# Two layers of attention with a memory: reads split in halves and put ahead of the value sums, low parts and feature sums on GpSimd, clipping on ScalarE

## The chip, the cores and the metric

One of the eight NeuronCores of a Trainium2 chip runs the whole program. The metric is the device time of one execution in microseconds (us), as a median over runs. The core has five engines, each with its own instruction stream that it works off in order: TensorE (PE, with its weight loads shown apart as PEld), VectorE (DVE), ScalarE (ACT), GpSimd (POOL) and SyncE (SP, which here only issues transfers and passes on syncs). They share an on-chip memory (SBUF); TensorE writes its results to eight banks of PSUM, from which VectorE and ScalarE read them.

## The reference

A sequence of 2048 rows of 512 features goes through four residual layers, A, B, A, B. Both have 32 heads of width 16. A is a linear attention with softmax features. B, the layer that the change touches, works on four segments of 512 rows one after the other:

```python
phi = lambda t: where(t > 0, t + 1.0, exp(t))
for s in range(4):                                   # segments of 512 rows
    logits = einsum("bhqd,bhkd->bhqk", qs, ks) * 0.25 + mask      # causal
    a_dot = einsum("bhqk,bhkd->bhqd", softmax(logits), vs)
    pq = phi(qs)
    a_mem = einsum("bhld,bhde->bhle", pq, M) / (einsum("bhld,bhd->bhl", pq, z)[..., None] + 1e-6)
    o = g * a_mem + (1 - g) * a_dot                  # g = sigmoid(beta), per head
    pk = phi(ks)
    M = M + einsum("bhld,bhle->bhde", pk, vs)        # the memory
    z = z + pk.sum over rows
```

In every segment but the first the queries read the memory of the segments before; in every segment but the last the keys and values are written to it. The result is in float32.

## The kernel before

**Number format.** Matrix products of wide operands are made of two parts of each operand, a rounded "hi" and the remainder "lo" (hi·hi + hi·lo + lo·hi). So every projected tile needs a cast (hi, ScalarE) and a subtraction (lo).

**Layer B's steps.** `LayerB.steps` writes out the order of the work by hand. A segment's 32 heads are 4 chunks `c` of 8 heads, a chunk is 2 halves, so a segment has 8 groups `m` of four heads, a layer 32. Each group takes five steps `k`; I call the five steps of a group's place a *turn*. The tables FIRST, GAPS, LAST and FINAL (first segment, middle ones, last of layer 1, last of layer 2) have one row per turn and one cell per step: `5.2` is step 2 of turn 5. The entries are jobs: `Q`, `V`, `O` (projections of queries and keys, of values, output), `a` (a read of the memory), `t`, `m` (the two parts of a write), `fin` (normalization of a group's value sums), `max`, `cv`, `n`, `ln` and others; `/6` means six pieces of such a job, and `+` means the next segment's. The order in which the program issues instructions to an engine is kept (`Ordered`, `held`), so an instruction that waits holds up all that stand behind it on its engine.

In each step the program issues, in this order: one of five products of logits of the group (`attend`), one of five sets of products for the row maxima of a group two turns ahead (`maxima`), functions that were put off to this step (`self.at`), stacking transfers (`stack`, in steps 2 and 4), in step 0 the value sums of the group before (`weighted`), and then the jobs of the table's cell.

- `attend`: TensorE writes logits to the tile `lg` (one buffer of two banks), ScalarE takes its exponential into a tile `P` (128 x 1024), and GpSimd sets what lies above the diagonal to zero (`affine_select`; 128 x 256 once or twice in steps 0 to 3, 128 x 512 in step 4).
- `maxima`: products in the banks `mx` and `my`, in steps 2 and 4 in two banks of the pool `g`; VectorE takes masked maxima (CUSTOM_DVE, then DVE_READ_ACCUMULATOR into `mxs`).
- `weighted`: 32 small matmuls `g<-P,v` in a bank of `g`, key blocks in the order 0, 3, 1, 2. Block 2 comes from the exponential of step 4. ScalarE copies the result out as `U`.
- `proj_pair`: queries and keys of one chunk, in steps 1 to 4 of turns 0, 1, 4 and 6, into two banks of `g`. Its matmuls come as two halves of rows that change places by syncs over SP. At the end ScalarE copies both out (`raw`, tile `tb`), and `projected` puts off the rest: `parts` (hi, lo) and `features` (phi). So the parts and the features of the projections fall into turns 1, 2, 5 and 7 (and the first step of the turn after).
- `reads`: two halves per chunk, each 64 matmuls `g<-mem,tb` in a bank of `g` and a normalization on VectorE into `ot`, to which `finish` adds the value sums.

The pool `g` has four banks (`G = 4`). They serve value sums, reads, projections, transposes and the maxima of steps 2 and 4. All this is issued through the helpers at lines 155 (every engine but TensorE), 177 (matmul) and 181 (transpose), so the profile shows tiles rather than lines.

In the kernel before, phi is made so: ScalarE `e = exp(raw)`; GpSimd `e = min(e, 1)`; then for keys GpSimd `raw = max(raw, 0)` and `e = e + raw`, for queries VectorE `e = max(raw, 0) + e` in one instruction, two steps later. With the projection's end in step 4, the query's parts, features and sum come 2, 4 and 6 steps later, the key's parts and features 3 and 5.

Of the kernel before, what the change touches and what calls it, by code (L numbers as in the profile page):

```python
# [7 lines left out]
F32 = mybir.dt.float32  # L8
# [56 lines left out]
7.0 m3 a0+ a0+ max fin | 7.1 V+/6 w | 7.2 V+/6 n        | 7.3 V+/6 n | 7.4 V+/6 w  # L65
# [12 lines left out]
0.0 a1 a1 max fin | 0.1 Q2/6 n cv3    | 0.2 Q2/6 n        | 0.3 Q2/6 n | 0.4 Q2/6  # L78
1.0 max turn fin | 1.1 Q3/6          | 1.2 Q3/6 n        | 1.3 Q3/6 | 1.4 Q3/6
2.0 max turn ln fin | 2.1 O/6          | 2.2 O/6           | 2.3 O/6 | 2.4 O/6  # L80
3.0 max turn turn fin ln | 3.1 O/6     | 3.2 O/6           | 3.3 O/6 | 3.4 O/6
4.0 a2 a2 max ln ln fin | 4.1 v/2 cv0  | 4.2 v/2           | 4.3 v/2 cv1 | 4.4 v/2
5.0 a3 a3 max fin | 5.1 v/2           | 5.2 v/2           | 5.3 v/2 | 5.4 v/2
6.0 max fin pre | 6.1 cv2         | 6.2 P/4           | 6.3 P/9 | 6.4 P/5 v/1
# [3 lines left out]
0.0 a1 a1 max fin | 0.1 Q2/6 cv3      | 0.2 Q2/6          | 0.3 Q2/6 | 0.4 Q2/6  # L88
1.0 max turn turn fin | 1.1 Q3/6       | 1.2 Q3/6          | 1.3 Q3/6 | 1.4 Q3/6
2.0 max fin | 2.1 O/6 cv0       | 2.2 O/6           | 2.3 O/6 | 2.4 O/6  # L90
3.0 a2 a2 max fin | 3.1 O/6           | 3.2 O/6           | 3.3 O/6 | 3.4 O/6
4.0 max turn turn fin | 4.1 O/6 cv1    | 4.2 O/6           | 4.3 O/6 | 4.4 O/6
5.0 a3 a3 max fin | 5.1 O/6           | 5.2 O/6           | 5.3 O/6 | 5.4 O/6
6.0 max fin pre | 6.1 cv2         | 6.2 P/4           | 6.3 P/9 | 6.4 P/5
# [7 lines left out]
def interleave_kernel(ctx, tc, x_in, a_wqkv, a_wphi, a_wo, b_wq, b_wk, b_wv, b_wo, b_beta,  # L102
# [878 lines left out]
    class LayerB:  # L981
# [53 lines left out]
        def proj_pair(self, s, c):  # L1035
# [344 lines left out]
        def steps(self, side, after, table_end):  # L1380
# [88 lines left out]
            for k in range(BEGIN, R * N + 1):  # L1469
# [110 lines left out]
```

## Time and profile before

| | |
|---|---|
| median of 3 runs | 1369.1 us (1363.52 to 1370.22) |
| profiled execution | 1368.14 us, of which the span is 1366.4 |
| granted TensorE clock, mean | 0.992 |
| PE busy | 1294.7 us (95%) |
| DVE busy | 1089.9 us (80%) |
| ACT busy | 809.1 us (59%) |
| POOL busy | 738.4 us (54%) |

In a row of the profile's groups stand: line, engine, operation, out<-in by the program's names with the shapes, count | busy time in us, mean duration in ns | idle time of the engine just before them in us, and what ended it. In the rows in order of time stand: start and duration in us, engine, line, operation, out<-in, shapes, count, and in brackets the idle time before and who ended it. A wait for several semaphores is put down to the one that the profile takes for the last. A matmul's end is modelled, and matmuls overlap.

The tile `lg` belongs to the logits, `mxs` to the maxima, `tb` to projected rows and features, `ta` to hi and lo, `mem` to the memory.

### The profile page before, as it was taken

What the parts mean: (1) busy time and instruction counts of PE and PEld (TensorE: products, weight loads), DVE (VectorE), ACT (ScalarE), POOL (GpSimd) and SP (SyncE); (2) the same over time, 40 slices, a digit from 0 to 9 for tenths busy, and PEclk for the clock granted to TensorE, in tenths of its full rate; (3) what the DMA queues carried; (4) which work ended last, traced back from release to release, by engine and by line L of the source; (5) the groups of instructions that cost most, each with busy time, mean ns of one, the idle gap of its engine ahead of it and who ended that gap; (6) DMA issues with size and microseconds to landing.
All of it is one profiled execution on the core that took longest, in us unless ns stands there. A gap on an engine that the chain in (4) does not pass through costs nothing.

```text
span 1366.4 us, 41853 instructions
## 1 busy us (share of the span) xinstructions
PE 1294.7 (95%) x16552; PEld 997.1 (73%) x16552; DVE 1089.9 (80%) x3327; ACT 809.1 (59%) x1202; POOL 738.4 (54%) x1084
## 2 busy tenths in 40 slices
PE   7999989999999999999999998999999999999987
PEld 6887868777667767767668886886767777677665
DVE  4766778778888989888767676787789889888885
ACT  5556345546777667667644433463667766766654
POOL 1568766426658558445324355563366666765443
PEclk9999999999999999999999998999999999999999
DMA  6398437534555544546351103655446554543432
GB/s 204 101 335 262 161 125 226 183 95 124 170 175 142 144 123 130 144 135 172 103 179 39 63 33 124 212 166 156 137 136 184 150 152 110 142 139 99 117 88 78
DMA packets 134420, 196.59 MB, mean 144 GB/s; under 512 B 15440, under 2 KB 61648, under 8 KB 133456
## 3 DMA queue, kind: packets, MB, share of 16 engines
q1 hardware_dynamic: 132256, 193.27, 47.1%
q8 instruction: 131, 2.15, 0.6%
q10 hardware_dynamic: 1968, 0.64, 0.2%
q14 instruction: 65, 0.53, 0.1%
HBM read 101.05 MB, written 39.85 MB: 103 GB/s over the span
## 4 chain that ended last, share of the span: by engine, by line
PE 57%; DVE 25%; issue 6%; ACT 5%; DMA 4%; POOL 2%; SPq 1%; DVEq 0%; ACTq 0%; POOLq 0%
PE g L177 46%; DVE g L155 4%; PE lg L177 3%; DVE mx L155 3%; DVE U L155 3%; DVE my L155 2%; DVE mxs L155 2%; PE mx L177 2%; PE g L181 2%; PE lg L181 2%; ACT P L155 2%; DVE ta L155 1%; DVE r L155 1%; DVE hl L155 1%; DVE tb L155 1%
## 5 line engine op out<-in xcount | busy, mean ns | idle before, releaser
L155 ACT ACTIVATE P<-lg 128x1024 f32<-128x1024 f32 x316 | 325.1, 1029 | 123.2 <-PE lg L177 85.2
L155 POOL TENSOR_SCALAR_AFFINE_SELECT P<-P 128x256 f32<-128x256 f32 (+1 forms) x448 | 204.6, 471 | 218.5 <-ACT P L155 216.3
L155 DVE CUSTOM_DVE_ANT_0 g<-g,mask 128x256 f32<-128x256 f32 (+3 forms) x392 | 189.8, 538 | 4.0 <-PE g L177 3.9
L177 PE MATMUL g<-hh,wqk 64*128 64x512 f32 (+1 forms) x960 | 181.6, 393 | 0.3
L177 PE MATMUL g<-w,oh 64*128 64x512 f32 (+2 forms) x848 | 171.6, 382 | 2.6 <-ACT oh L155 2.6
L177 PE MATMUL g<-P,v 128*32 128x128 f32 (+3 forms) x2064 | 151.7, 433 | 18.6 <-DVE mxs L155 17.8
L155 DVE CUSTOM_DVE_ANT_0 mx<-mx,mask 128x512 f32<-128x512 f32 (+2 forms) x316 | 158.1, 500 | 12.2 <-PE my L177 10.3
L155 DVE CUSTOM_DVE_ANT_0 my<-my,mask 128x512 f32<-128x512 f32 (+2 forms) x316 | 163.2, 517 | 0.0
L177 PE MATMUL lg<-e,e 64*128 64x512 f32 (+1 forms) x1010 | 149.3, 341 | 11.4 <-ACT P L155 10.5
L177 PE MATMUL g<-w,hh 64*128 64x512 f32 (+1 forms) x672 | 143.2, 394 | 2.1 <-ACT w L155 1.3
L155 DVE DVE_READ_ACCUMULATOR2_ANT mxs<- 128x1 f32 x1024 | 142.0, 139 | 0.0
L177 PEld LDWEIGHTS g<-P,v 128*32 128x32 f32 x2064 | 63.0, 109 | 101.4 <-issue 60.8
L177 PEld LDWEIGHTS lg<-e,e 64*128 64x128 f32 x1010 | 97.1, 185 | 47.2 <-ACT P L155 21.8
L155 POOL TENSOR_SCALAR tb<-tb 128x512 f32<-128x512 f32 x72 | 108.7, 1521 | 16.0 <-ACT tb L155 8.0
L177 PEld LDWEIGHTS g<-w,oh 64*128 64x128 f32 (+1 forms) x848 | 104.2, 187 | 16.7 <-ACT oh L155 3.5
L177 PE MATMUL g<-w,ol 64*128 64x512 f32 (+2 forms) x424 | 112.6, 378 | 0.0
L177 PEld LDWEIGHTS g<-hh,wqk 64*128 64x128 f32 (+1 forms) x960 | 97.6, 185 | 19.4 <-ACT hh L155 1.4
L177 PE MATMUL g<-hl,wqk 64*128 64x512 f32 (+1 forms) x480 | 100.8, 392 | 1.6 <-DVE hl L155 1.6
L155 POOL TENSOR_TENSOR ot<-ot,wt 128x256 f32<-128x256 f32 x46 | 34.0, 739 | 121.5 <-DVE wt L155 121.5
L177 PEld LDWEIGHTS g<-w,hh 64*128 64x128 f32 (+1 forms) x672 | 83.5, 188 | 16.4 <-ACT w L155 1.6
L155 ACT COPY tb<-g 128x512 f32<-128x512 f32 (+1 forms) x132 | 71.1, 576 | 39.7 <-PE g L177 36.2
L177 PE MATMUL mx<-e,e 63*128 63x384 f32 (+3 forms) x323 | 89.2, 337 | 2.9 <-ACT mt L155 2.0
(164 smaller groups left out, 2962.0 us busy)
## 6 DMA issues: line engine op xcount, KB each, us to landing
e<-ta SPq DMA_DIRECT2D x384, 128.0 KB
wqk<-wqk SPq DMA_DIRECT2D x128, 256.0 KB
x<-x SPq DMA_DIRECT2D x48, 256.0 KB
pq<-tb SPq DMA_DIRECT2D x24, 256.0 KB
tb<-pq SPq DMA_DIRECT2D x24, 256.0 KB
x<-xr SPq DMA_DIRECT2D x22, 256.0 KB
xr<-x SPq DMA_DIRECT2D x20, 256.0 KB
x<-in SPq DMA_DIRECT2D x16, 256.0 KB
```

The source lines that it names most:

```text
L155: i = f(*a, **k)
L177: return held(nc.tensor.matmul(*a, **k))
L181: return held(nc.tensor.transpose(*a))
```

## The change

Three things are changed.

1. *Reads.* In the tables the two halves of a chunk's read now stand in two turns, one each, instead of two in one turn (chunk 3 had one in each of two turns already in the middle segments). They carry a `<`, and jobs with a `<` are done in step 0 before `weighted` instead of after it. Chunk 0 is read in turn 7 of the segment before and turn 0, chunk 1 in turns 1 and 2, chunk 2 in 3 and 4, chunk 3 in 5 and 6.
2. *Low parts.* From step 5 on the subtraction for lo runs on GpSimd instead of VectorE.
3. *Features.* ScalarE computes `e = relu(-raw)` and `e = exp(-e)`, which is min(exp(raw), 1), so GpSimd's minimum goes. For keys ScalarE also does `raw = relu(raw)`; for queries GpSimd does `raw = max(raw, 0)`. The sum runs on GpSimd for both. The query's parts, features and sum come 2, 3 and 4 steps after the projection's end, the key's 3, 5 and 6.

```diff
 GAPS = """
-0.0 a1 a1 max fin | 0.1 Q2/6 n cv3    | 0.2 Q2/6 n        | 0.3 Q2/6 n | 0.4 Q2/6
-1.0 max t0 turn fin | 1.1 Q3/6      | 1.2 Q3/6 n        | 1.3 Q3/6 | 1.4 Q3/6
-2.0 m0 max turn t1 fin ln | 2.1 O/6    | 2.2 O/6           | 2.3 O/6 | 2.4 O/6
-3.0 m1 max turn turn fin ln | 3.1 O/6  | 3.2 O/6           | 3.3 O/6 | 3.4 O/6
-4.0 a2 a2 max ln ln fin | 4.1 Q0+/6 cv0  | 4.2 Q0+/6       | 4.3 Q0+/6 cv1 | 4.4 load begin Q0+/6
-5.0 a3 max t2 fin | 5.1 V+/6 | 5.2 V+/6 n N      | 5.3 V+/6 n N | 5.4 V+/6
-6.0 m2 a3 max t3 fin | 6.1 Q1+/6 cv2   | 6.2 Q1+/6 n N     | 6.3 Q1+/6 n N | 6.4 Q1+/6
-7.0 m3 a0+ a0+ max fin | 7.1 V+/6      | 7.2 V+/6 n N      | 7.3 V+/6 n N | 7.4 V+/6
+0.0 <a0 max fin | 0.1 Q2/6 n cv3    | 0.2 Q2/6 n        | 0.3 Q2/6 n | 0.4 Q2/6
+1.0 <a1 max t0 turn fin | 1.1 Q3/6      | 1.2 Q3/6 n        | 1.3 Q3/6 | 1.4 Q3/6
+2.0 <a1 m0 max turn t1 fin ln | 2.1 O/6    | 2.2 O/6           | 2.3 O/6 | 2.4 O/6
+3.0 <a2 m1 max turn turn fin ln | 3.1 O/6  | 3.2 O/6           | 3.3 O/6 | 3.4 O/6
+4.0 <a2 max ln ln fin | 4.1 Q0+/6 cv0  | 4.2 Q0+/6       | 4.3 Q0+/6 cv1 | 4.4 load begin Q0+/6
+5.0 <a3 max t2 fin | 5.1 V+/6 | 5.2 V+/6 n N      | 5.3 V+/6 n N | 5.4 V+/6
+6.0 <a3 m2 max t3 fin | 6.1 Q1+/6 cv2   | 6.2 Q1+/6 n N     | 6.3 Q1+/6 n N | 6.4 Q1+/6
+7.0 <a0+ m3 max fin | 7.1 V+/6      | 7.2 V+/6 n N      | 7.3 V+/6 n N | 7.4 V+/6
...
@@ proj_pair
-                for n, f in zip((2, 4, 6) if m == 0 else (3, 5), job):
+                for n, f in zip((2, 3, 4) if m == 0 else (3, 5, 6), job):
...
@@ projected
-                dve.tensor_tensor(out=lo, in0=raw, in1=hi.bitcast(F32), op=SUB)
+                (pool if self.k >= R else dve).tensor_tensor(out=lo, in0=raw, in1=hi.bitcast(F32), op=SUB)
...
                 def features():
-                    act.activation(e, raw, AF.Exp)
-                    pool.tensor_scalar(e, e, 1.0, None, op0=MIN)
+                    act.activation(e, raw, AF.Relu, scale=-1.0)
+                    act.activation(e, e, AF.Exp, scale=-1.0)
                     if m == 1:
+                        act.activation(raw, raw, AF.Relu)
+
+                def added():
+                    if m == 0:
                         pool.tensor_scalar(raw, raw, 0.0, None, op0=MAX)
-                        pool.tensor_tensor(out=e, in0=e, in1=raw, op=ADD)
-
-                def added():
-                    dve.scalar_tensor_tensor(out=e, in0=raw, scalar=0.0, in1=e, op0=MAX, op1=ADD)
-                todo += [features] + [added] * (m == 0)
+                    pool.tensor_tensor(out=e, in0=raw, in1=e, op=ADD)
+                todo += [features, added]
...
@@ steps
+                what, s = table.get(k, ((), 0))
+                for w in what:
+                    if w[0] == "<":
+                        do(w[1:], s, k)
                 if k % R == 0 and 0 <= k // R - 1 < N:
                     self.weighted(k // R - 1)
...
-                what, s = table.get(k, ((), 0))
                 for w in what:
-                    do(w, s, k)
+                    if w[0] != "<":
+                        do(w, s, k)
```

The other three tables are changed in the same way: FIRST has only `<a0+` in 7.0, LAST and FINAL have the same seven halves in turns 0 to 6.

More of the change, by code (lines that the diff above doesn't have):

```diff
@@ L64 @@
 6.0 m2 max t3 fin | 6.1 Q1+/6 cv2   | 6.2 Q1+/6 n       | 6.3 Q1+/6 n | 6.4 Q1+/6 w
-7.0 m3 a0+ a0+ max fin | 7.1 V+/6 w | 7.2 V+/6 n        | 7.3 V+/6 n | 7.4 V+/6 w
+7.0 <a0+ m3 max fin | 7.1 V+/6 w | 7.2 V+/6 n        | 7.3 V+/6 n | 7.4 V+/6 w
 """
 GAPS = """
-0.0 a1 a1 max fin | 0.1 Q2/6 n cv3    | 0.2 Q2/6 n        | 0.3 Q2/6 n | 0.4 Q2/6
-1.0 max t0 turn fin | 1.1 Q3/6      | 1.2 Q3/6 n        | 1.3 Q3/6 | 1.4 Q3/6
-2.0 m0 max turn t1 fin ln | 2.1 O/6    | 2.2 O/6           | 2.3 O/6 | 2.4 O/6
@@ L76 @@
+7.0 <a0+ m3 max fin | 7.1 V+/6      | 7.2 V+/6 n N      | 7.3 V+/6 n N | 7.4 V+/6
 """
 LAST = """
[L78 to L82, printed above, removed]
@@ L83 @@
-5.0 a3 a3 max fin | 5.1 v/2           | 5.2 v/2           | 5.3 v/2 | 5.4 v/2
-6.0 max fin pre | 6.1 cv2         | 6.2 P/4           | 6.3 P/9 | 6.4 P/5 v/1
+0.0 <a0 max fin | 0.1 Q2/6 n cv3    | 0.2 Q2/6 n        | 0.3 Q2/6 n | 0.4 Q2/6
+1.0 <a1 max turn fin | 1.1 Q3/6          | 1.2 Q3/6 n        | 1.3 Q3/6 | 1.4 Q3/6
+2.0 <a1 max turn ln fin | 2.1 O/6          | 2.2 O/6           | 2.3 O/6 | 2.4 O/6
+3.0 <a2 max turn turn fin ln | 3.1 O/6     | 3.2 O/6           | 3.3 O/6 | 3.4 O/6
+4.0 <a2 max ln ln fin | 4.1 v/2 cv0  | 4.2 v/2           | 4.3 v/2 cv1 | 4.4 v/2
@@ L85 @@
+5.0 <a3 max fin | 5.1 v/2           | 5.2 v/2           | 5.3 v/2 | 5.4 v/2
+6.0 <a3 max fin pre | 6.1 cv2         | 6.2 P/4           | 6.3 P/9 | 6.4 P/5 v/1
 7.0 max fin | 7.1 P/4           | 7.2 P/5 v/1       | 7.3 P/4 v/1 | 7.4 P/5 v/2
@@ L87 @@
 FINAL = """
[L88 to L94, printed above, removed]
+0.0 <a0 max fin | 0.1 Q2/6 cv3      | 0.2 Q2/6          | 0.3 Q2/6 | 0.4 Q2/6
+1.0 <a1 max turn turn fin | 1.1 Q3/6       | 1.2 Q3/6          | 1.3 Q3/6 | 1.4 Q3/6
+2.0 <a1 max fin | 2.1 O/6 cv0       | 2.2 O/6           | 2.3 O/6 | 2.4 O/6
+3.0 <a2 max fin | 3.1 O/6           | 3.2 O/6           | 3.3 O/6 | 3.4 O/6
+4.0 <a2 max turn turn fin | 4.1 O/6 cv1    | 4.2 O/6           | 4.3 O/6 | 4.4 O/6
+5.0 <a3 max fin | 5.1 O/6           | 5.2 O/6           | 5.3 O/6 | 5.4 O/6
+6.0 <a3 max fin pre | 6.1 cv2         | 6.2 P/4           | 6.3 P/9 | 6.4 P/5
 7.0 max fin | 7.1 P/4           | 7.2 P/5           | 7.3 P/4 | 7.4
```

## The prediction

> **What bounds the kernel now.** I read the page first, then the two stretches in which the attention layer's steps run, then the waits of TensorE, then one turn in order of time.
>
> ```profile
> PE 1294.7 (95%) x16552; PEld 997.1 (73%) x16552; DVE 1089.9 (80%) x3327; ACT 809.1 (59%) x1202; POOL 738.4 (54%) x1084
> ```
> ```profile
> 300.00:690.00 390.00, 371.47 (x5472) 277.31 (x5472) 337.35 (x1224) 269.65 (x389) 221.48 (x367) 1.00 0.51 143
> 930.00:1345.00 415.00, 391.95 (x5676) 292.31 (x5674) 357.87 (x1311) 273.90 (x398) 229.56 (x380) 1.00 0.47 131
> ```
> The second view gives, for each stretch, the busy time of PE, PEld, DVE, ACT and POOL. The change touches only these 805 us. There TensorE is busy 763.4 us, so it idles 41.6 us, and no change of its waits can win more than that. VectorE is busy 695.2 us (86%), ScalarE 543.6 (68%), Pool 451.0 (56%).
>
> ```profile
> PEld g L177 <- POOL P L155: 36.9, 59, 1.4
> ```
> ```profile
> PE g L177 <- DVE mxs L155: 19.3, 35, 1.0
> PE lg L177 <- ACT P L155: 10.5, 20, 1.3
> ```
> The largest wait seems to be that of the value sums' weight loads for Pool's selects. One turn shows who really ends it (segment 1, steps 2 to 4 of turn 5, then step 0 of turn 6):
>
> ```profile
> 461.30 1.03 ACT L155 ACTIVATE P<-lg 128x1024 f32<-128x1024 f32 x1 [0.46 <-POOL ot L155]
> 462.23 0.61 ACT L155 CAST ta<-tb 128x512 fp32r<-128x512 f32 x1
> 463.21 1.03 ACT L155 ACTIVATE P<-lg 128x1024 f32<-128x1024 f32 x1 [0.37 <-POOL P L155]
> 464.13 0.62 ACT L155 ACTIVATE tb<-tb 128x512 f32<-128x512 f32 x1
> 465.12 1.03 ACT L155 ACTIVATE P<-lg 128x1024 f32<-128x1024 f32 x1 [0.36 <-POOL P L155]
> ```
> ```profile
> 464.31 0.77 POOL L155 TENSOR_SCALAR_AFFINE_SELECT P<-P 128x256 f32<-128x256 f32 x2 [1.11 <-ACT P L155]
> 465.05 1.50 POOL L155 TENSOR_SCALAR tb<-tb 128x512 f32<-128x512 f32 x1
> 466.50 0.63 POOL L155 TENSOR_SCALAR_AFFINE_SELECT P<-P 128x512 f32<-128x512 f32 x1
> ```
> ```profile
> 464.61 0.40 PE L177 MATMUL lg<-e,e 64*128 64x256 f32 x4
> ...
> 466.47 0.39 PE L177 MATMUL lg<-e,e 64*128 64x512 f32 x2
> 466.70 0.39 PE L177 MATMUL mx<-e,e 63*128 63x512 f32 x1
> ```
> ```profile
> 467.74 0.14 DVE L155 DVE_READ_ACCUMULATOR2_ANT mxs<- 128x1 f32 x1
> ```
> ```profile
> 467.99 0.19 PEld L177 LDWEIGHTS g<-P,v 128*32 128x32 f32 x8 [1.32 <-POOL P L155]
> ```
> The select of step 4 ended at 467.13; the value sums began at 467.99, which is 0.11 after VectorE's third maximum of step 4 was read out (467.74 + 0.14). So they wait for a PSUM bank "g" that the maxima still hold: VectorE is late, not Pool.
>
> **The change, part by part.** Prices come from these groups:
>
> ```profile
> L155 POOL TENSOR_SCALAR tb<-tb 128x512 f32<-128x512 f32 x72 | 108.7, 1521 | 16.0 <-ACT tb L155 8.0 <-DMA e<-ta 8.0
> L177 PE MATMUL g<-P,v 128*32 128x512 f32 x504 | 67.1, 602 | 18.6 <-DVE mxs L155 17.8 <-POOL mmq L155 0.6 <-POOL P L155 0.2
> L155 DVE TENSOR_TENSOR ta<-tb,ta 128x512 fp32r<-128x512 f32 x64 | 44.2, 690 | 15.1 <-ACT ta L155 15.1
> L177 PE MATMUL g<-mem,tb 128*32 128x34 f32 x3072 | 34.6, 198 | 4.0 <-issue 3.5
> L155 POOL TENSOR_TENSOR tb<-tb,tb 128x512 f32<-128x512 f32 x24 | 31.3, 1305 | 2.0
> L155 POOL TENSOR_TENSOR ol<-U,oh 128x512 fp32r<-128x512 f32 x24 | 30.9, 1286 | 9.7 <-ACT oh L155 8.8
> L155 ACT ACTIVATE tb<-tb 128x512 f32<-128x512 f32 x48 | 29.9, 623 | 0.0
> L155 DVE SCALAR_TENSOR_TENSOR tb<-tb,tb 128x512 f32<-128x512 f32 x24 | 21.4, 893 | 0.0
> ```
> *Work moved.* 56 of the 64 low parts leave VectorE (the four per layer before step 5 stay), and so do all 24 query sums: 56 x 0.690 + 24 x 0.893 = 60.0 us less. Pool loses 48 minima and 24 key clips, and gains 24 query clips, 24 query sums and 56 low parts, these at the price of the like subtraction "ol": it had 108.7 + 31.3 = 140.0 us and gets 24 x 1.521 (query clips) + 48 x 1.305 (sums) + 56 x 1.286 = 171.1, so +31.1. ScalarE gains one pass per query and two per key chunk, 72 x 0.623 = +44.9 us; a Relu is not in the trace and I price it as the Exp of the same shape. Averages say nothing yet, since VectorE has the least room and the other two have some; what counts is which wait ends last.
>
> *VectorE's bank wait.* The group of the value sums waits 17.8 us for "mxs". The longest of these waits is 1.0 us; in each turn that follows a projection of Q and K, VectorE now sheds two subtractions, 2 x 0.69 = 1.38 us, ahead of step 4's maxima, and a sum in the next turn. That covers such a wait whole. The turns ahead of the value and output rows shed a sum, or half of a pair of reads. The last turns of each layer have no projections and shed nothing, so I keep 2.8 us. Gain **15** (bounds 0 and 17.8). Moving a read ahead does not itself remove this wait: the read needs a "g" bank too and would take the very one.
>
> *The reads.* 48 halves, 34.6 / 48 = 0.72 us each, are only moved; what goes is the 4.0 us that they idle when two stand in a row and share banks. Gain **3** (0 and 4.0). Earlier reads also let VectorE and ScalarE start what hangs on them; of the 10.5 us that TensorE waits for exponentials, which are late in part because ScalarE itself waits for VectorE (the idle 0.79 in the rows below), I take **3** (0 and 10.5).
>
> *ScalarE in step 2.* That lateness on ScalarE reaches TensorE, because the products have one "lg" buffer, is shown where a cast and a normalization stand between two exponentials (ScalarE's rows, then the product that waited):
>
> ```profile
> 504.12 0.62 ACT L155 CAST oh<-U 128x512 fp32r<-128x512 f32 x1 [0.79 <-DVE U L155]
> 504.64 0.82 ACT L155 ACTIVATE x<-x,st 128x512 f32<-128x512 f32 x1
> 505.36 1.00 ACT L155 ACTIVATE P<-lg 128x1024 f32<-128x1024 f32 x1
> ```
> ```profile
> 506.42 0.39 PE L177 MATMUL lg<-e,e 64*128 64x256 f32 x2 [0.63 <-ACT P L155]
> ```
> A pass hands the engine on 0.52 us after its start (504.12 to 504.64), and a product starts 0.06 after its exponential's end (506.36 to 506.42). Now two query passes stand in step 2 ahead of the key's cast: in the turn above Relu at 462.23, Exp 462.75, cast 463.27 to 463.88, and the exponential of step 3 at 463.79 instead of 463.21, ending at 464.82. The product of step 4 began at 464.61 and now cannot before 464.88: the margin of 0.37 us is used up and 0.27 lost, in each of 24 turns with query features: loss **7** (bounds 0, and 24 x 0.63 = 15 by the row at 506.42). The key's three passes stand in step 4; with them and two copies of projections the exponential of step 0 ends near 465.4 + 0.92 + 5 x 0.52 + 1.03 = 470.0. The next product comes after the value sums, which by the next paragraph are then in their fourth block, so I price the passes at nothing; without that room the two added ones would cost 1.04 us a time.
>
> *Pool between steps 2 and 4.* Who waits for the select of step 4?
>
> ```profile
> 520.40 0.16 PEld L177 LDWEIGHTS g<-P,v 128*32 128x32 f32 x8 [0.35 <-issue]
> ...
> 521.83 0.13 PEld L177 LDWEIGHTS g<-P,v 128*32 128x32 f32 x4 [0.19 <-issue]
> ```
> ```profile
> 684.86 0.64 POOL L155 TENSOR_SCALAR_AFFINE_SELECT P<-P 128x512 f32<-128x512 f32 x1 [1.29 <-ACT P L155]
> ...
> 685.27 0.16 PEld L177 LDWEIGHTS g<-P,v 128*32 128x32 f32 x8 [0.24 <-issue]
> ```
> Only the fourth key block of the value sums reads it, 1.43 us after their start (521.83 against 520.40); and at 685.27 they did start before their select had ended (685.50). In the turn above the cast now ends at 463.88, so the low part runs from 463.95 to 465.24, the select of step 3 (0.77) to 466.01, the clip (1.50) to 467.51, the sum (1.30) to 468.81, and the select of step 4 (0.63), which stands behind them, to 469.44. TensorE, with steps as before, has the product of step 0 at 464.88 + 1.86 = 466.74, the maxima 0.23 later, a read some 0.3 after these (the idle 0.35 of the first row), the value sums 0.72 later at 468.0 and the fourth block at 469.43. That is the moment at which the select ends: the read is exactly the cover. For some spread of Pool's durations I set 0.15 us for 22 turns; the two that end at turn 6 of segment 0 have no read ahead and pay 0.72: loss **5** (0, and 24 x 0.72 = 17 if the cover is worth nothing).
>
> The Trainium skill (GPSIMD Engine Reference, section 4.1, Engine selection) says that an elementwise instruction with one input runs on Pool at about line rate and that two inputs make it about twice as slow; its section 3.1 measures 769 ns for 512 elements of a tight loop. The trace disagrees: the clip with one input takes 1.52 us, more than the sum with two (1.31). By the page the chain would be 0.7 us shorter, the loss of 5 would be gone and the sum would be -14 instead of -9; the trace decides.
>
> *Queues.* The query's stacking transfers now wait in SP's queue for Pool's low part, 1.29 instead of 0.69 us and behind the select of step 1; the syncs that order TensorE's row halves stand behind them in SP. The next such sync is needed two steps (2 x 1.86 us) later, so this is hidden; with Pool 3 us later it would not be.
>
> **Sum.** -15 - 3 - 3 + 7 + 5 = -9 us. Against the profiled execution's own 1368.14 (span 1366.4 plus 1.74) that is 1359; the median of the runs, 1369.1, lies 1 us above it, so **1360**.
>
> **Rivals.**
> *Slower: Pool's chain decides.* Place: the select of step 4 in the 24 query turns. It decides as soon as the chain is later than the fourth block; the slack is nothing, so each 0.1 us costs 2.4 us. Without the loss of 5 the kernel would stand at 1355; 0.6 us a turn eats the gain, and from 0.9 us it is slower by more than can be taken for noise. At 1 us: 1355 + 24 = 1379; if the value sums needed the select at their start (1.43 us), 1355 + 34 = 1389. For it: the wait labelled POOL P, 59 times, and low part, clip and sum where one clip stood. Against: the start at 685.27.
> *No difference.* The bank wait moves to the read and only half goes (-7.5), the other gains fail, the losses stay: +4.5, 1374. For it: the read needs the same bank. Against: VectorE sheds more than the longest wait.
> *Larger gain.* ScalarE's earlier idle time and Pool's lighter load in step 0 (one sum instead of three instructions) leave both losses out: -21, 1348.
> *Relu costs a table load.* The trace has a single load:
>
> ```profile
> L655 ACT ACT_TABLE_LOAD x1 | 1.3, 1283 | 2.3 <-issue 2.3
> ```
> If each change between Relu and Exp made one, some 96 loads of 1.28 us would add 123 us: 1483. Copy, Identity, Ln and Exp alternate without any. The Trainium skill (ScalarE: Activation LUTs, Table sets) says that relu is in every set; no run here shows a Relu yet.
>
> **How the numbers follow.** Forecast 0.40, slower by Pool 0.20, no difference 0.25, larger gain 0.13, table loads 0.02. A measurement of this kernel tells about 0.5% (7 us) from no change. Faster by more: most of the forecast (0.32), the larger gain (0.13) and a little of the third (0.05), 0.50. Slower: 0.16 of Pool's case, the loads, and 0.02 of the third, 0.20. The rest 0.30. The forecast's own range is 1350 to 1368; with the cases of either side it is 1345 to 1385.
>
> **What would show it.** Right: the value sums' idle behind "mxs" falls from 17.8 to under 5 us; VectorE's busy time falls by some 60, Pool's rises by 31, ScalarE's by 45; the product of step 4 starts 0.3 us later in query turns, behind ACT P. The select of step 4 ends close to the fourth block. Wrong: gaps inside the value sums ahead of the fourth block, behind POOL P, of 0.5 us and more; reads that now idle behind "mxs"; exponentials late by more than one pass.

## The result, and the profile after

The changed kernel takes 1359.92 us (median of 8 runs, 1355.09 to 1361.87) against 1368.47 for the kernel before (8 runs, 1363.52 to 1370.22): a ratio of 0.9938 with a 95% interval of 0.9919 to 0.9957. The forecast was 1360. The number held; the experiments below show that most of the terms that make it up did not.

The page of the kernel after, busy time of each engine:

```profile
PE 1295.2 (95%) x16552; PEld 990.1 (73%) x16552; DVE 1045.2 (77%) x3247; ACT 841.5 (62%) x1274; POOL 751.4 (55%) x1116
```

The same stretches as before (their ends don't fall on quite the same work, since the kernel is shorter), with the busy time of PE, PEld, DVE, ACT and POOL:

```profile
300.00:690.00 390.00, 377.53 (x5468) 278.99 (x5467) 317.15 (x1183) 284.13 (x422) 235.96 (x391) 1.00 0.51 143
930.00:1345.00 415.00, 396.55 (x5732) 291.87 (x5730) 334.56 (x1263) 291.55 (x434) 239.59 (x394) 1.00 0.46 128
```

TensorE idles 30.9 us in them (805 - 377.53 - 396.55) instead of 41.6. Its waits, in us in total, times, longest:

```profile
PE lg L177 <- ACT P L155: 12.6, 38, 1.6
PEld g L177 <- POOL P L155: 13.1, 41, 0.8
PE g L177 <- DVE mxs L155: 4.9, 11, 0.9
```

The wait for VectorE's maxima has gone from 19.3 to 4.9, that for the exponentials has risen from 10.5 to 12.6. The groups that answer to those of before (busy, mean ns, idle before and who ended it):

```profile
L155 ACT ACTIVATE tb<-tb 128x512 f32<-128x512 f32 x120 | 72.9, 625 | 3.3 <-DVE ta L155 1.8
L155 POOL TENSOR_TENSOR ta<-tb,ta 128x512 fp32r<-128x512 f32 x56 | 72.2, 1290 | 16.5 <-ACT ta L155 15.7
L177 PE MATMUL g<-P,v 128*32 128x512 f32 x504 | 67.6, 606 | 0.9 <-DVE mxs L155 0.9
L155 POOL TENSOR_TENSOR tb<-tb,tb 128x512 f32<-128x512 f32 x48 | 61.9, 1289 | 19.8 <-ACT tb L155 17.8
L177 PE MATMUL g<-P,v 128*32 128x256 f32 x536 | 42.7, 380 | 0.3 <-POOL P L155 0.2
L177 PE MATMUL g<-mem,tb 128*32 128x34 f32 x3072 | 37.2, 200 | 3.2 <-DVE mxs L155 3.1
L155 POOL TENSOR_SCALAR tb<-tb 128x512 f32<-128x512 f32 x24 | 35.7, 1489 | 0.0
L655 ACT ACT_TABLE_LOAD x1 | 1.3, 1283 | 2.3 <-issue 2.3
```

The prices of single instructions were right: Relu and Exp together 625 ns a pass (0.623 us forecast) and still a single table load, the low part 1290 ns on Pool (1286 forecast), the sum 1289 (1305), the clip 1489 (1521). The busy times of the engines moved less than was forecast: VectorE's by -44.7 us (-60), ScalarE's by +32.4 (+45), Pool's by +13.0 (+31). Part of that is the way of counting: busy time counts neighbouring instructions that overlap only once (ScalarE's groups before sum to 864.3 us, its busy time is 809.1). On Pool the selects of 128 x 256 also became shorter, 409 instead of 443 ns, 12.9 us in all; why, no run shows. The value sums wait 0.9 us for "mxs" instead of 17.8, and the reads, now ahead of them, wait 3.1.

### The profile page after: what moved, and what is told of

Read it like the earlier page. It is cut to its first block, busy times and chain, and to the rows that moved or that the text cites. A ratio compares the mean times of both kernels' runs of the same rounds, so it can differ in the third digit from the quotient of the medians.

```text
span 1358.8 us, 41839 instructions
## 1 busy us (share of the span) xinstructions
PE 1295.2 (95%) x16552; PEld 990.1 (73%) x16552; DVE 1045.2 (77%) x3247; ACT 841.5 (62%) x1274; POOL 751.4 (55%) x1116
## 4 chain that ended last, share of the span: by engine, by line
PE 67%; DVE 14%; ACT 8%; POOL 4%; issue 3%; DMA 2%; SPq 1%; DVEq 0%; ACTq 0%; POOLq 0%
PE g L177 52%; PE lg L177 6%; ACT P L155 4%; PE mx L177 3%; PE g L181 3%; DVE U L155 2%; PE lg L181 2%; DVE g L155 2%; POOL P L155 1%; POOL tb L155 1%; ACT ta L155 1%; DVE mx L155 1%; DVE es L155 1%; PE my L177 1%; DVE hl L155 1%
## 5 line engine op out<-in xcount | busy, mean ns | idle before, releaser
L155 POOL TENSOR_SCALAR_AFFINE_SELECT P<-P 128x256 f32<-128x256 f32 (+1 forms) x448 | 191.3, 442 | 197.2 <-ACT P L155 194.6
L155 DVE CUSTOM_DVE_ANT_0 g<-g,mask 128x256 f32<-128x256 f32 (+3 forms) x392 | 190.6, 542 | 17.9 <-PE g L177 17.8
L177 PE MATMUL lg<-e,e 64*128 64x512 f32 (+1 forms) x1010 | 151.3, 345 | 13.2 <-ACT P L155 12.6
L177 PE MATMUL g<-w,hl 64*128 64x512 f32 (+1 forms) x336 | 89.4, 393 | 0.0
```

What stands on the lines that cost most here:

```text
L155: i = f(*a, **k)
L177: return held(nc.tensor.matmul(*a, **k))
```

## The experiments

Each kernel has runs of the kernel before beside it, on the same chip. Their medians differ a little (1367.39 to 1369.23), so I compare ratios, and turn them into us as (ratio - 1) x 1368.5. An interval is about 3 us to either side, and that of a difference between two rows about 4.

The last column is a second measure, from the one profiled execution of each kernel: the time from the start of the first exponential (`P<-lg`) of a layer B to that of its last, both layers added, against the kernel before (290.17 to 694.87 and 956.84 to 1352.21, 800.1 us). It leaves out most of the work that the change doesn't touch, and has no interval. Profiles also differ where the kernels are the same: at one and the same copy of ScalarE in the first layer A, which no kernel here changes, the profile of the whole change is already 2.0 us ahead (183.53 against 185.51).

| kernel | median, us (range) | ratio to before, 95% | us against before | first to last exponential, us against before |
|---|---|---|---|---|
| reads part alone | 1355.42 (1353.31 to 1357.54) | 0.9913 [0.9896, 0.993] | -11.9 | -8.4 |
| low parts alone | 1357.01 (1354.9 to 1360.63) | 0.9926 [0.9908, 0.9944] | -10.1 | -7.5 |
| features part alone | 1367.3 (1365.0 to 1373.53) | 0.9998 [0.9982, 1.0015] | -0.3 | +2.4 |
| low + features | 1367.59 (1363.48 to 1376.34) | 1.0004 [0.9987, 1.0022] | +0.5 | +4.9 |
| reads + low | 1353.6 (1352.04 to 1360.25) | 0.9908 [0.9889, 0.9927] | -12.6 | -12.7 |
| reads + features | 1363.03 (1359.7 to 1369.25) | 0.9964 [0.9947, 0.998] | -4.9 | -0.7 |
| whole change | 1359.92 (1355.09 to 1361.87) | 0.9938 [0.9919, 0.9957] | -8.5 | -3.7 |
| whole, query's features later | 1359.08 (1355.94 to 1361.2) | 0.9941 [0.9924, 0.9957] | -8.1 | -5.1 |
| whole, Pool's query clip twice | 1387.65 (1386.68 to 1392.31) | 1.0156 [1.0136, 1.0176] | +21.3 | +25.0 |
| reads spread, behind the value sums | 1355.11 (1354.39 to 1356.1) | 0.9904 [0.9881, 0.9928] | -13.1 | -10.4 |
| reads in pairs, ahead of the value sums | 1384.99 (1382.87 to 1385.58) | 1.0119 [1.0098, 1.014] | +16.3 | +18.4 |
| reads + low + the keys' features | 1348.97 (1347.21 to 1351.52) | 0.986 [0.9839, 0.9882] | -19.2 | -17.8 |
| reads + low + the queries' features | 1371.1 (1366.51 to 1373.62) | 1.0011 [0.9998, 1.0025] | +1.5 | +3.3 |

In all rows but one the second measure stands 1.4 to 4.8 us above the first (for the whole change -3.7 against -8.5), so some 3 us of it seem to belong to the one execution of the kernel before. Rows compared with each other are safer, and there the two measures agree within the noise. Below, us are by the medians where nothing else is said.

### The three parts, each alone

**Reads alone** (the tables and the two loops in `steps`, nothing else).

> The kernel before with the reads alone split and moved ahead of the value sums. Theory (the value sums wait for a bank that VectorE holds, so the read that now comes first takes over the wait): the idle behind mxs moves from g<-P,v (17.8 us) to g<-mem,tb, the sum of the two stays above 14 us, and the time falls by 0 to 4 us, to 1364 to 1368. Rival (the value sums wait for Pool's select, and the read covers it): the wait goes, 1354 to 1358.

It gains 11.9 us by itself, where my theory said at most 4, and keeps only part of the bank wait. The groups of the kernel with the reads part alone:

```profile
L177 PE MATMUL g<-P,v 128*32 128x512 f32 x504 | 68.0, 608 | 4.2 <-DVE mxs L155 4.2
L177 PE MATMUL g<-mem,tb 128*32 128x34 f32 x3072 | 37.4, 200 | 5.8 <-DVE mxs L155 5.8
L155 DVE TENSOR_SCALAR r<-g 128x16 f32<-128x16 f32 x48 | 8.3, 173 | 0.0
```

Value sums and reads together wait 10.0 us for "mxs", not 17.8, and VectorE no longer stands idle ahead of the addition of eps (`r<-g`), which the read releases. In the kernel before that row was:

```profile
L155 DVE TENSOR_SCALAR r<-g 128x16 f32<-128x16 f32 x48 | 8.2, 171 | 28.1 <-PE g L177 28.1
```

So I formed a theory: before, VectorE's next instructions depended on a read that TensorE had queued behind the value sums, so VectorE stood still for 28.1 us and came late to the next maxima; the order ahead of the value sums cures that. It explains the numbers so far. It is wrong, as two runs further down show.

**Low parts alone.**

```diff
-                dve.tensor_tensor(out=lo, in0=raw, in1=hi.bitcast(F32), op=SUB)
+                (pool if self.k >= R else dve).tensor_tensor(out=lo, in0=raw, in1=hi.bitcast(F32), op=SUB)
```

> The kernel before with the low parts alone on GpSimd from step 5 on. Theory: VectorE sheds 38.6 us, 1.38 us in each turn with the parts of a projection, which is most of the relief; the idle of the value sums behind mxs falls from 17.8 to under 8 us, Pool's chain (low part, select, minimum, select) still ends before the fourth key block; 1355 to 1361. Rival (Pool is the engine that is waited for): 56 x 1.29 us more on Pool come out as waits, 1372 or more.

The groups of that kernel, the value sums:

```profile
L177 PE MATMUL g<-P,v 128*32 128x512 f32 x504 | 67.1, 603 | 7.5 <-DVE mxs L155 6.7 <-POOL mmq L155 0.6
```

The wait for "mxs" falls from 17.8 to 6.7, by 11.1 us, and the kernel gains 10.1, as the theory said. This is the prediction's mechanism in its pure form: VectorE sheds 56 subtractions, the bank comes free earlier, TensorE starts earlier by about the same amount.

**Features alone** (with the steps 2, 3, 4 and 3, 5, 6 of the change).

```diff
-                    act.activation(e, raw, AF.Exp)
-                    pool.tensor_scalar(e, e, 1.0, None, op0=MIN)
+                    act.activation(e, raw, AF.Relu, scale=-1.0)
+                    act.activation(e, e, AF.Exp, scale=-1.0)
...
-                    dve.scalar_tensor_tensor(out=e, in0=raw, scalar=0.0, in1=e, op0=MAX, op1=ADD)
+                    if m == 0:
+                        pool.tensor_scalar(raw, raw, 0.0, None, op0=MAX)
+                    pool.tensor_tensor(out=e, in0=raw, in1=e, op=ADD)
```

> The kernel before with the features' part alone (clipping on ScalarE, sums on GpSimd, the new steps). Theory: VectorE sheds 21.4 us (bank wait down by 3 to 7), ScalarE's two passes ahead of the cast cost 0.27 us in 24 turns (7 us), and Pool's clip and sum end the select of step 4 about 0.3 us after the fourth key block without a read ahead (7 us): +5 to +12, 1373 to 1380. Rival (VectorE's relief decides, the rest is hidden): 1361 to 1365.

Nothing is gained and nothing lost; the time lies between the theory's and the rival's. The waits of that kernel show an exchange:

```profile
PE lg L177 <- ACT P L155: 15.1, 42, 1.6
PE g L177 <- DVE mxs L155: 14.7, 29, 1.0
```

TensorE waits 4.6 us less for VectorE (19.3 before), and 4.6 us more for ScalarE's exponentials (10.5 before).

### Two parts at a time

**Low and features, without the reads.**

> The whole change without the reads' part: low parts and features moved, reads where they were before. Theory (the read ahead is exactly the cover of Pool's chain): the bank wait is gone (-15), ScalarE costs 7, and the select of step 4 comes 0.7 us after the fourth key block in 24 turns (17 us), a wait for POOL P inside the value sums: +5 to +12, 1374 to 1380. Rival (Pool's chain has room, the reads matter little): within 3 us of the whole change, 1358 to 1363.

**Reads and low.**

> Reads and low parts as in the change, features as before (minimum, key clip and key sum on GpSimd, query sum on VectorE). Theory: VectorE's relief of 38.6 us without ScalarE's extra passes (7 us) and without the longer Pool chain (5 us): 1350 to 1356, faster than the whole change. Rival (the features' part carries a good share of the gain): slower than the whole change, 1362 or more.

**Reads and features.**

> Reads and features as in the change, low parts on VectorE as before. Theory: relief of 21.4 us only, bank wait down by 3 to 7 us, ScalarE costs 7, Pool's chain without the low part is covered by the read: -5 to +3, 1363 to 1371. Rival (low parts on GpSimd cost as much as they bring): within 3 us of the whole change, 1357 to 1363.

Reads gain 11.9 and low parts 10.1, but both together only 12.6: two cures for one lateness, of which the second adds 0.7 by the medians and 4.3 by the second measure. The theory for reads and low parts came true, that for reads and features at the edge of its range; low parts and features came out at 1367.6, between theory and rival. The features cost wherever there is something to lose: 7.0 us on top of the reads (-11.9 to -4.9), 10.6 on top of the low parts (-10.1 to +0.5), 4.1 on top of both (-12.6 to -8.5). Without the reads in front of the value sums some idle time shows ahead of the fourth key block; the group of the fourth key block in the kernel with low parts and features:

```profile
L177 PE MATMUL g<-P,v 128*32 128x256 f32 x536 | 42.3, 384 | 2.9 <-POOL P L155 0.3
```

2.9 us of idle time there (only 0.3 of it put down to Pool), 0.3 with the reads ahead. If the read covers anything, it is little: 17 us were expected.

### How much room has Pool's chain?

The whole change, with the query's clip done twice (the second is idempotent): 24 x 1.49 = 35.8 us more on Pool, in the chain between steps 2 and 4, and nothing else.

```diff
                     if m == 0:
                         pool.tensor_scalar(raw, raw, 0.0, None, op0=MAX)
+                        pool.tensor_scalar(raw, raw, 0.0, None, op0=MAX)
```

> The whole change with GpSimd's clip of the query rows done twice (the result is the same), 1.49 us more in 24 turns ahead of the select of step 4. Theory (the chain ends when the fourth key block starts, slack nothing): 24 x 1.49 = 36 us at most, 1388 to 1397 with a wait for POOL P in the value sums. Rival (the select has a slack of 1 us or more): under 12 us, 1360 to 1372.

The group of the fourth key block in that kernel:

```profile
L177 PE MATMUL g<-P,v 128*32 128x256 f32 x536 | 42.6, 384 | 26.2 <-POOL P L155 26.2
```

It costs 29.8 us (1.0156 - 0.9938 of 1368.5), that is 1.24 of the 1.49 us in each turn, and 26.2 us of it stand in that row. So the chain has a slack of about 0.25 us (0.1 to 0.4 with the interval), and past that it decides, just as the prediction's rival said. The slack is on the side of the matmuls: the weight loads `g<-P,v` wait 13.1 us for Pool's `P` in the changed kernel and 48.9 with the second clip, the whole 35.8 more. In the changed kernel itself the chain doesn't decide: 0.3 us in all.

### Can the query's passes on ScalarE be hidden in other steps?

The whole change with the query's parts, features and sum 2, 4 and 6 steps after the projection, as in the kernel before, instead of 2, 3 and 4.

```diff
-                for n, f in zip((2, 3, 4) if m == 0 else (3, 5, 6), job):
+                for n, f in zip((2, 4, 6) if m == 0 else (3, 5, 6), job):
```

> The whole change, with the query's parts, features and sum 2, 4 and 6 steps after the projection instead of 2, 3 and 4. Theory: ScalarE has one cast in step 2 and two passes in step 3 (where 0.36 us were idle) instead of three passes in step 2, and clip and sum stand behind the select of step 4: the losses of 7 and 5 us shrink to 2 and 0, 1348 to 1354. Rival (neither was a loss, the gain is what VectorE sheds): as the whole change, 1358 to 1362.

The time doesn't move (0.9941 against 0.9938), and the exponentials are no earlier. The wait of that kernel:

```profile
PE lg L177 <- ACT P L155: 15.6, 25, 1.7
```

Fewer waits than the 38 of the changed kernel, each longer. My theory that step 2 was the wrong place, and that another would give the loss back, fell. The rival's time came, but not its reason: the wait for the exponentials is still a loss.

### What in the reads part gains: the order or the spreading?

**Spread, but behind the value sums:** the changed tables without the `<`, in the kernel before.

```diff
-0.0 a1 a1 max fin | 0.1 Q2/6 n cv3    | 0.2 Q2/6 n        | 0.3 Q2/6 n | 0.4 Q2/6
-1.0 max t0 turn fin | 1.1 Q3/6      | 1.2 Q3/6 n        | 1.3 Q3/6 | 1.4 Q3/6
+0.0 a0 max fin | 0.1 Q2/6 n cv3    | 0.2 Q2/6 n        | 0.3 Q2/6 n | 0.4 Q2/6
+1.0 a1 max t0 turn fin | 1.1 Q3/6      | 1.2 Q3/6 n        | 1.3 Q3/6 | 1.4 Q3/6
...
```

> The kernel before with only the reads' places changed: one half a turn (turns 0 to 6, as in the change) instead of two halves in some turns, but still behind the value sums in TensorE's order. Theory (the order decides: VectorE stands still because the read that it needs is queued behind the value sums, and that stays so here): VectorE's idle time ahead of the addition of eps (28.1 us before) stays over 20 us, the value sums' wait for mxs stays over 14 of 17.8 us, and only the 4.0 us that the reads idle behind one another can go: 1363 to 1368. Rival (the spreading decides, one bank less asked for at a time): as fast as the reads part whole, 1354 to 1358, with the value sums' wait for mxs under 7 us.

**In pairs as before, but ahead of the value sums:** the `<` in the tables of the kernel before.

```diff
-0.0 a1 a1 max fin | 0.1 Q2/6 n cv3    | 0.2 Q2/6 n        | 0.3 Q2/6 n | 0.4 Q2/6
+0.0 <a1 <a1 max fin | 0.1 Q2/6 n cv3    | 0.2 Q2/6 n        | 0.3 Q2/6 n | 0.4 Q2/6
...
```

> The kernel before with only the reads' order changed: two halves in a turn as before, both queued ahead of the value sums. Theory (the order decides): VectorE's idle time ahead of the addition of eps falls from 28.1 us to under 3, and the time to 1354 to 1360; the second half of a pair may still wait for a bank that the maxima hold, so the sum of TensorE's waits for mxs ahead of reads and value sums falls to about 10 us, as with the reads part whole. Rival (the spreading decides): the pair takes both banks while the maxima hold them, the wait moves to the reads at its full size (some 20 us behind mxs) and the time stays at 1364 to 1369.

The theory of the order fell. Spreading alone gives -13.1 us, the whole gain of the reads part; the order ahead adds nothing that shows. The tables of this run also put a read ahead of the matmuls of the write (`m`) in its turn; in turn 6, where nothing else changed, the distance in the table below stays the same (4.66 and 4.71). Two signs of the theory did come, VectorE's idle time over 20 us and a bank wait over 14, but not its time; of the rival the time came, but not its bank wait under 7. The weight loads of the value sums still wait 34.6 us for Pool's `P` there (36.9 before, 9.3 with the reads ahead), so the rival of the first run, that the read covers Pool's select, doesn't explain the gain either. The groups of the kernel with the reads spread behind the value sums:

```profile
L177 PE MATMUL g<-P,v 128*32 128x512 f32 x504 | 67.1, 602 | 15.8 <-DVE mxs L155 14.2 <-POOL mmq L155 0.6 <-POOL st L155 0.3
L177 PE MATMUL g<-mem,tb 128*32 128x34 f32 x3072 | 37.6, 198 | 0.0
L155 DVE TENSOR_SCALAR r<-g 128x16 f32<-128x16 f32 x48 | 8.4, 174 | 46.2 <-PE g L177 46.1
```

VectorE's idle time there did not shrink, it rose to 46.2 us, and the kernel is as fast as the one where it is 0.0: so no cost of this idle time shows. Even the bank wait is still 14.2 of 17.8. What goes is something that the rows of before show if one looks at the weight loads, which TensorE issues ahead of the matmuls. Two places of the kernel before, in order of time, turn 7 of segment 1 and turn 0 of segment 2; TensorE's rows:

```profile
483.70 1.17 PE L177 MATMUL g<-mem,tb 128*32 128x34 f32 x107
486.07 0.38 PE L177 MATMUL g<-mem,tb 128*32 128x34 f32 x20 [1.20 <-issue]
...
498.05 1.22 PEld L177 LDWEIGHTS g<-mem,tb 128*32 128x32 f32 x128 [0.60 <-DVE tb L155]
498.06 1.33 PE L177 MATMUL g<-mem,tb 128*32 128x34 f32 x128
```

the row of VectorE that ends the second wait:

```profile
496.97 1.03 DVE L155 SCALAR_TENSOR_TENSOR tb<-tb,tb 128x512 f32<-128x512 f32 x1
```

and the group of the reads' weight loads, still of the kernel before:

```profile
L177 PEld LDWEIGHTS g<-mem,tb 128*32 128x32 f32 x3072 | 32.5, 108 | 8.9 <-issue 4.2 <-DVE tb L155 2.9
```

In turn 7 the second half of a pair stops for 1.20 us after 108 of 128 matmuls. In turn 0 the pair of chunk 1 stands in the very step in which VectorE makes that chunk's query features (496.97 to 498.00, and the read starts at 498.05); with one half a turn chunk 1 is read a turn later and the wait isn't there. The pairs ahead of the value sums lose 16.3 us, slower than both theory and rival, and they lose it here; the group of the reads in that kernel:

```profile
L177 PE MATMUL g<-mem,tb 128*32 128x34 f32 x3072 | 34.5, 201 | 18.9 <-DVE tb L155 12.3 <-DVE mxs L155 5.5 <-issue 1.0
```

Put ahead, they wait for that sum six times, some 2 us each, 12.3 in all, and their idle time grows by 14.9 (4.0 before). The wait for "mxs" ahead of the value sums falls at the same time (17.8 to 5.7), so idle times alone don't add up to the loss. Its place is clear all the same: from the exponential of step 0 to that of step 1 in turn 0, the six segments that read take 13.8 us longer than before. So this kernel doesn't test the order by itself; the one with the spread reads does.

The exponentials of steps 0 and 1 enclose the value sums and the reads. Turn 7 of segment 1 in the kernel before, ScalarE's rows in order of time:

```profile
481.14 1.04 ACT L155 ACTIVATE P<-lg 128x1024 f32<-128x1024 f32 x1
...
487.19 1.03 ACT L155 ACTIVATE P<-lg 128x1024 f32<-128x1024 f32 x1 [0.22 <-PE lg L177]
```

That is 6.05 us. By such rows, as a mean of the four middle segments (those with the table GAPS), the distance is, in turns 0 to 7, before and with the spread reads:

| turn | 0 | 1 | 2 | 3 | 4 | 5 | 6 | 7 | sum |
|---|---|---|---|---|---|---|---|---|---|
| halves read before | 2 | 0 | 0 | 0 | 2 | 1 | 1 | 2 | 8 |
| before, us | 4.56 | 3.04 | 3.71 | 3.51 | 4.70 | 3.88 | 4.66 | 5.21 | 33.27 |
| one half a turn, us | 3.40 | 3.52 | 4.41 | 4.00 | 4.12 | 3.89 | 4.71 | 3.69 | 31.74 |

A half adds 0.48 to 0.70 where it comes, and its leaving takes 0.58 to 1.52. The difference is 1.53 us a middle segment. Over all turns of both layers this distance falls by 10.1 us in sum, nearly the whole 10.4 of the second measure; the other 2.5 of the 12.9 us between the two profiles (spans of 1366.4 and 1353.5) lie in stretches without reads. By the groups, at most 4.0 us are the stops inside the pairs, 2.9 the waits for the query's sum, and 3.6 the smaller bank wait (17.8 to 14.2), 10.5 together. That split is read off the rows and was not tried one by one.

### Which half of the features part costs?

Reads and low parts whole, and of the features only the keys' half (three passes on ScalarE, the sum on Pool a step later, as in the change, and not two as the expectation below says; queries as before):

```diff
-                    act.activation(e, raw, AF.Relu, scale=-1.0)
-                    act.activation(e, e, AF.Exp, scale=-1.0)
-                    if m == 1:
+                    if m == 0:
+                        act.activation(e, raw, AF.Exp)
+                        pool.tensor_scalar(e, e, 1.0, None, op0=MIN)
+                    else:
+                        act.activation(e, raw, AF.Relu, scale=-1.0)
+                        act.activation(e, e, AF.Exp, scale=-1.0)
...
```

> The reads part and the low parts whole, and of the features part only the keys' half: three passes on ScalarE in step 4 and the sum on Pool two steps later; the queries' features stay as before (one pass on ScalarE, minimum on Pool, sum on VectorE). Theory (what the features part costs is the queries' extra pass on ScalarE in step 2 and Pool's longer chain behind it): as fast as reads and low parts together, 1350 to 1356, with TensorE's wait lg for ACT P at about 9 us. Rival (it is the keys' two extra passes in step 4, which the prediction priced at nothing): 1357 to 1361, and that wait rises to about 13 us.

and only the queries' half (Relu and Exp on ScalarE, clip and sum on Pool; keys as before, with minimum, clip and sum on Pool):

```diff
                 def features():
-                    act.activation(e, raw, AF.Relu, scale=-1.0)
-                    act.activation(e, e, AF.Exp, scale=-1.0)
                     if m == 1:
-                        act.activation(raw, raw, AF.Relu)
+                        act.activation(e, raw, AF.Exp)
+                        pool.tensor_scalar(e, e, 1.0, None, op0=MIN)
+                        pool.tensor_scalar(raw, raw, 0.0, None, op0=MAX)
+                        pool.tensor_tensor(out=e, in0=e, in1=raw, op=ADD)
+                    else:
+                        act.activation(e, raw, AF.Relu, scale=-1.0)
+                        act.activation(e, e, AF.Exp, scale=-1.0)
...
```

> The reads part and the low parts whole, and of the features part only the queries' half: Relu and Exp on ScalarE in step 2, clip and sum on Pool in step 3; the keys' features stay as before (one pass on ScalarE, minimum, clip and sum on Pool). Theory (the cost lies with the queries): 1357 to 1362, with TensorE's wait lg for ACT P at 12 to 15 us as in the whole change. Rival (the cost lies with the keys' passes): 1351 to 1355, with that wait at about 9 us.

The cost lies with the queries, and by more than I expected; the keys' half gains, which I had not expected. From reads and low parts (-12.6) the keys' half leads to -19.2, the fastest kernel of the study, and the queries' half to +1.5. The same wait with reads and low parts only, with the keys' half and with the queries' half:

```profile
PE lg L177 <- ACT P L155: 8.7, 19, 1.2
```
```profile
PE lg L177 <- ACT P L155: 7.0, 17, 1.2
```
```profile
PE lg L177 <- ACT P L155: 19.0, 43, 2.4
```

The single longest wait of the kernel with the queries' half is 2.45 us. Its rows in turn 0 of segment 2, Pool, then VectorE, ScalarE and TensorE:

```profile
497.41 2.95 POOL L155 TENSOR_SCALAR tb<-tb 128x512 f32<-128x512 f32 x2
500.44 1.43 POOL L155 TENSOR_TENSOR tb<-tb,tb 128x512 f32<-128x512 f32 x1
501.83 0.48 POOL L155 TENSOR_TENSOR st<-st 128x4 f32<-128x4 f32 x2
...
503.81 0.75 POOL L155 TENSOR_TENSOR ot<-ot,wt 128x256 f32<-128x256 f32 x1
```
```profile
504.59 0.71 DVE L155 STREAM_TRANSPOSE U<-ot 128x512 f32<-128x512 f32 x1 [2.33 <-POOL ot L155]
```
```profile
505.33 0.62 ACT L155 CAST oh<-U 128x512 fp32r<-128x512 f32 x1 [2.60 <-DVE U L155]
505.86 0.81 ACT L155 ACTIVATE x<-x,st 128x512 f32<-128x512 f32 x1
506.58 1.00 ACT L155 ACTIVATE P<-lg 128x1024 f32<-128x1024 f32 x1
```
```profile
507.63 0.50 PE L177 MATMUL lg<-e,e 64*128 64x256 f32 x4 [2.45 <-ACT P L155]
```

The key's minimum, clip and sum (4.38 us) stand on Pool ahead of the small normalization work and of `ot`, the addition that finishes a group; the query's longer chain has pushed all of them back. VectorE transposes `ot`, ScalarE casts it, and the exponential of step 3 stands behind that cast in ScalarE's queue. So ScalarE idles 2.60 us for Pool, and TensorE 2.45 for ScalarE. The keys' half takes two of the key's three instructions off Pool, and this wait is gone: in the changed kernel the longest wait for the exponentials is 1.6, and their sum falls from 19.0 to 12.6. With reads and low parts only, the same wait is there too, but smaller:

```profile
500.89 0.50 PE L177 MATMUL lg<-e,e 64*128 64x256 f32 x4 [0.84 <-ACT P L155]
```

It comes in turn 0 of segment 2 in both layers (0.84 and 0.86) and is gone with the keys' half. That makes 1.7 us (8.7 to 7.0) of the 6.6 that the keys' half gains there; where the rest comes from, these runs don't show.

## Why the prediction was right, and where it was not

**The sum.** Forecast -15 - 3 - 3 + 7 + 5 = -9, measured -8.5. Built up part by part the runs give -11.9 (reads), -0.7 (low parts on top), -6.6 (the keys' features), +10.7 (the queries' features). The gains, 21 us forecast, are 19.2; the losses, 12 forecast, are 10.7. That both sides come out so near is luck: what makes them up is different. The reads bring four times their term, the low parts on top of them little, the keys' features, priced at nothing, bring 6.6, and of the losses Pool's 5 are missing while ScalarE's are larger. The shares also hang on the order: put on first, the queries' half costs 14.1 (-12.6 to +1.5) and the keys' half then brings 10.0.

**VectorE's bank wait: -15.** The reading of the row was right, that VectorE and not Pool ends this wait: low parts alone take 11.1 us from it and gain 10.1. But nearly the same gain comes from spreading the reads, which leaves 14.2 us of the wait standing. On top of the reads the low parts add 0.7 (4.3 by the second measure), and the wait's disappearance (17.8 to 0.9, forecast under 5) is not what the 8.5 us are made of alone. The sign of error that the prediction named, reads that idle behind "mxs", did come, but with 3.1 us.

**The reads: -3.** This is the term that failed most: "what goes is the 4.0 us that they idle when two stand in a row". The 4.0 did go, but the part is worth 11.9 by itself. I had not looked at what the pairs wait for in the weight loads' row, and I priced the move of a half as neutral, while in the middle segments a second half in the same turn costs 0.58 to 1.52 us and a single one 0.48 to 0.70. The sentence that "moving a read ahead does not itself remove this wait" holds only in part: with the reads ahead, value sums and reads together still wait 10.0 of 17.8.

**ScalarE in step 2: +7.** Right in place and mechanism, somewhat small. In the turn shown before, the same rows after the change, ScalarE:

```profile
458.40 1.03 ACT L155 ACTIVATE P<-lg 128x1024 f32<-128x1024 f32 x1 [0.50 <-PE lg L177]
459.32 1.29 ACT L155 ACTIVATE tb<-tb 128x512 f32<-128x512 f32 x2
460.51 0.60 ACT L155 CAST ta<-tb 128x512 fp32r<-128x512 f32 x1
461.02 1.02 ACT L155 ACTIVATE P<-lg 128x1024 f32<-128x1024 f32 x1
462.69 1.03 ACT L155 ACTIVATE P<-lg 128x1024 f32<-128x1024 f32 x1 [0.66 <-PE lg L177]
```

and the product that waited:

```profile
462.09 0.50 PE L177 MATMUL lg<-e,e 64*128 64x256 f32 x4 [0.23 <-ACT P L155]
```

Two passes and the cast stand between the exponentials as forecast, and the product waits 0.23 (0.27 forecast). From the exponential of step 2 to that of step 4 it takes 4.29 us instead of 3.82 (465.12 - 461.30), so 0.47 is lost, not 0.27. By the like rows of the other turns of this segment it is 0.2 in turn 1 and 0.46 to 0.49 in turns 2 and 7, some 1.6 us a segment, and 10 us over the 24 turns.

**The key's three passes: nothing, hidden behind the value sums.** No loss, as forecast, but the term was not nothing: the keys' half gains 6.6. The rival of a larger gain had named Pool's lighter load in step 0. One path of it is shown in rows, over `ot`, the cast and the exponential behind it. TensorE's whole wait for the exponentials falls by 1.7 us on top of reads and low parts, and by 6.4 on top of the queries' half (19.0 to 12.6); the rest of the 6.6 stays open.

**Pool's chain between steps 2 and 4: +5.** The select of step 4 and the row of the value sums' fourth block, after the change, Pool and TensorE's weight loads:

```profile
465.99 0.63 POOL L155 TENSOR_SCALAR_AFFINE_SELECT P<-P 128x512 f32<-128x512 f32 x1
```
```profile
466.67 0.43 PEld L177 LDWEIGHTS g<-P,v 128*32 128x32 f32 x8 [0.22 <-POOL P L155]
```

The select ends at 466.62 and the block starts at 466.67: the coincidence that was forecast. The weight loads' idle 0.22 hides behind matmuls that are still running, so the block's own row loses 0.3 us in all, and the 5 are nothing. The rival on the slower side named the right place and the right slope: a slack of 0.25 us, then 1.24 us lost for 1.49 added.

**Exponentials late: -3.** Wrong in sign for the whole change (10.5 to 12.6): the queries' half alone takes this wait from 8.7 to 19.0. With reads, low parts and the keys' half it is right (7.0, that is -3.5).

**Relu.** One table load as before. The Trainium skill (ScalarE: Activation LUTs, Table sets) says that relu is in every set; these runs, with 72 Relu passes between the Exp passes, agree.

## What to carry to other kernels

Price each part of a change against the state that the other parts leave: two cures of one lateness (-11.9 and -10.1) gave -12.6, and a part that measured nothing alone held a gain of 6.6 and a loss of 10.7 that runs with one half at a time brought apart. And look at the steps that a change touches as well as at the whole: profiles of kernels that are the same in a layer differed by 2.0 us there. Idle time that an engine off the path loses in front of a wait is no proof that the wait costs anything; here VectorE's 28 us in the kernel before became 0 in one kernel and 46 in another, and both were some 12 us faster; only a run that spread the reads and left them behind the value sums told which of the two mattered. When work is added to an engine that works in order, follow what stands behind it through every engine's queue to the one that sets the end: work on Pool reached TensorE over an addition, a transpose, a cast and an exponential.

## What the hardware showed that I had not expected

A long row of small matmuls can stop without a cause that the profile names. In the pairs of reads of the kernel before TensorE stopped in the middle five times, 0.32 to 1.20 us, after a run of small matmuls with a weight load each that takes some 11 ns a pair (107 in 1.17 us); with one half a turn it never did. With the pairs ahead, the value sums behind a pair stop in their turn (turn 0 of segment 2: their weight loads idle 1.01 us up to 504.29, with no cause named). The two longest, 1.20 and 0.93, stand in turn 7, where 32 value sums and 32 matmuls of a write come right before the pair. The Trainium skill (Runtime: NRT & Kernel Launch, Instruction fetch mechanics) says that an engine's instructions are fetched in blocks ahead of use, and that this is hidden because instructions are issued slowly; whether these stops are that fetch, no run here shows.
